# Chunked attention, MoE and routed MoE on one core: ones spread on the chip, `a` loaded once, the first unit's states emitted sooner, and 64 small products of zeros around TensorE's first work

## Chip, cores and metric

One Trainium2 chip, one core. The metric is device time in microseconds (us) of one execution. Each kernel is run several times; the profile is of one more execution of the same program, and its rows are in microseconds from the start of its span.

## What is computed

Three layers follow one another on 4 x 768 = 3072 tokens. The change lies in the start of the first.

```python
def _attn_ref(x, a, B, C):          # batch 4, 8 heads, 768 steps, head_dim 32, d_state 16, chunks of 32
    log_a = np.log(np.clip(a, 1e-06, 1.0))
    for c in range(nc):
        cum = np.cumsum(la, axis=-1)
        M = (C B^T) * exp(cum_i - cum_j) * causal
        y = M @ x + (C @ state) * exp(cum)
        state = exp(sum(la)) * state + sum_j B_j x_j exp(cum_last - cum_j)
def _moe_ref(x, w_gate, w_val, w_out):      # 256 -> 1536 -> 256
    return silu(x @ w_gate) * (x @ w_val) @ w_out
def _moe2_ref(...):                          # 8 experts, 256 -> 1024 -> 256, top 1
    e_idx = np.argmax(x @ w_gate + modality_bias[modality_id], axis=1)
    out[mask] = gate_w[mask, None] * (np.maximum(x[mask] @ w1[e], 0.0) @ w2[e])
```

## The kernel before

The tokens lie in 6 blocks of 512. A block has 4 units of 128 steps (`NU` = 24 units), and a unit holds all 8 heads. The attention of a unit is built from small TensorE products: `scores_mm` (lines 293 and 299) makes the sums for the state and the scores `pc`, `scores_m` (307) masks the scores, `states` (317 to 329) carries the state, `values_mm` (345 and 355) makes `py`, `values_out` (371 to 376) multiplies by the decays `U` and rounds into `xt`, and `values_low` (382) keeps the remainder of that rounding. Weights of the first MLP come as 64-bit numbers in strips of 768 KB (`load_w`, line 393) and are taken apart by `decode`: ScalarE makes `ha` (405) and `wv` (408), VectorE joins them (414, then 418), ScalarE makes the high part `wh` (421), VectorE or GpSimd the low part `wl` (423). The MLP's products (`mlp1_mm`, line 443) can begin when block 0's `xt` and strip 0 are complete.

`first_block` (from line 808) writes out by hand the order in which every engine gets its work, under a manual schedule. It loads, takes the logarithm of `a` (`setup_ln`, 184 and 185), makes the decay weights `W` (`setup_decay`, 189 and 190) and the running sums `er` (`setup_cum`, 196 and 198), weighs unit 0 with `W` (`weigh`, 280) and then goes through the four units of block 0, with four, four and six idle products (`keep_busy`, 207) in between. `cum_split` (225, 228) splits `er`, `setup_ones` (217, 218) copies two matrices of ones out of the constants `c1`, `emit_d` (261, GpSimd) spreads `er` into `du`, `emit_u` (272, 273) multiplies `du` by the ones into `U`, and `cum_ends_d`, `cum_ends` and `cum_store` (233, 240, 245) make the factors `eb` that `states` needs.

Loads are issued from SyncE (SP) in the order of the code; `c1` is issued from ScalarE in two pieces. `at` holds `a` twice side by side, because `setup_cum` wants both copies as its stationary operand. `raw` has three buffers, for the weight strips. PSUM tiles come from pools: tag `a` with 3 buffers (`pc`, `py`), tag `g` with 3 (`pw`, `pe`, `pu`, later the MLP), and two `y` banks, one of which `keep_busy` writes.

Of the kernel before, what the change touches and what calls it, by code (L numbers as in the profile page):

```python
# [9 lines left out]
F32 = mybir.dt.float32  # L10
# [20 lines left out]
NBLK = T // BLK  # L31
# [5 lines left out]
C_S = 0  # L37
C_ME = C_S + 132
C_MU = C_ME + 1
C_R16 = C_MU + 8  # L40
C_R32 = C_R16 + 128
C_MK = C_R32 + 256
C1 = C_MK + 64
C_ID = C1
C_TRI = C_ID + 128
# [9 lines left out]
def _consts():  # L55
    k = np.arange(128)[:, None]
    j = np.arange(128)[None, :]
    c = np.zeros((128, C_END), np.float32)

    same = k // 64 == j // 64  # L60
    m = np.zeros((128, 128), np.float32)
    m[same & (k % 64 < 32) & (k > j)] = 1.0
    m[same & (k % 64 >= 32) & (k <= j)] = -1.0
    c[:, C_S:C_S + 128] = m
    for q, (lo, hi) in enumerate(((32, 96), (96, 128), (0, 32))):
        c[lo:hi, C_S + 128 + q] = -1.0
    r = np.arange(128)
    c[:, C_ME] = (r // 32) % 2
    for q in range(8):
        c[:, C_MU + q] = 4 * (r // 64) + (r // 8) % 4 == q  # L70
    c[:, C_R16:C_R16 + 128] = (r % 8)[:, None] == j // 16
    for g in range(2):
        c[:, C_R32 + 128 * g:C_R32 + 128 * g + 128] = (r % 8)[:, None] == 4 * g + j // 32
    c[:, C_MK:C_MK + 64] = j[:, :64] >= k % 64
    c[:, C_ID:C_ID + 128] = k == j
    c[:, C_TRI:C_TRI + 128] = k < j
    e = np.arange(E)
    c[:, C_IE:C_IE + 8] = 8 - e
    for g, (b0, n) in enumerate(GROUPS):
        c[:, C_EC + 8 * g:C_EC + 8 * g + 8] = E * b0 * BLK + e * (n * BLK)  # L80
    c[:, C_LE:C_LE + 64] = (e[None, :] <= e[:, None]).reshape(1, 64)
    c[:, C_TT:C_TT + 11] = np.arange(11)
    c[:, C_KK:C_KK + 4] = np.arange(4) * BLK
    c[:, C_IO:C_IO + 8] = e
    return c


def _layout(inp):
    o = {}
    at = inp["a"].reshape(NB * NH, NC, 128).reshape(NB, NH, NC, 128).transpose(3, 0, 2, 1)  # L90
    at = at.reshape(128, NBLK, 1, 32)
    o["at"] = np.broadcast_to(at, (128, NBLK, 2, 32)).reshape(128, NBLK, 64)
    xk = inp["x"].reshape(NB, NH, NC, 128, D).transpose(3, 0, 2, 1, 4).reshape(128, NU, DM)
    bk = inp["B"].reshape(NB, NH, NC, 128, N).transpose(3, 0, 2, 1, 4).reshape(128, NU, 128)
    bt = inp["B"].reshape(NB, NH, NC, 128, N).transpose(1, 4, 0, 2, 3).reshape(128, NU, 128)
    o["xbb"] = np.concatenate([xk, bk, bt], axis=2)

    ct = inp["C"].reshape(NB, 2, 4, NC, 2, 64, N).transpose(1, 2, 6, 0, 3, 4, 5).reshape(2, 4, N, NU, 2, 64)
    cd = np.zeros((2, 4, N, NU, 2, 4, 64), np.float32)
    for h in range(4):  # L100
        cd[:, h, :, :, :, h] = ct[:, h]
    o["cbd"] = cd.reshape(128, NU, 512)
    o["cst"] = _consts()

    def bits(w):
        return np.ascontiguousarray(w).view(np.int64)

    wg = bits(inp["moe_w_gate"]).reshape(2, 128, NF, 128).transpose(2, 1, 0, 3)
    wv = bits(inp["moe_w_val"]).reshape(2, 128, NF, 128).transpose(2, 1, 0, 3)
    wo = bits(inp["moe_w_out"]).reshape(NF, 128, DM)  # L110
    o["mw"] = np.concatenate([wg.reshape(NF, 128, 256), wv.reshape(NF, 128, 256), wo], axis=2)
    o["mid"] = np.ascontiguousarray(inp["moe2_modality_id"]).reshape(NU, 128).T
    o["wl"] = inp["moe2_w_gate"].reshape(2, 128, E).transpose(1, 0, 2)
    o["mb"] = np.broadcast_to(inp["moe2_modality_bias"].reshape(1, 2, E), (128, 2, E))
    w1 = inp["moe2_w1"].reshape(E, 2, 128, F2).transpose(0, 2, 1, 3).reshape(E, 128, 2 * F2)
    w2 = inp["moe2_w2"].reshape(E, NF2, 128, DM).transpose(0, 2, 1, 3).reshape(E, 128, NF2 * DM)
    o["ew"] = np.concatenate([w1, w2], axis=2).reshape(E * 128, 4096)
    return {k: np.ascontiguousarray(v) for k, v in o.items()}
# [3 lines left out]
def kernel(  # L122
# [23 lines left out]

    c1 = ap_.tile([128, C1], F32, name="c1")
    c2 = keep.tile([128, C_END - C1], F32, name="c2")
    at = ap_.tile([128, NBLK, 64], F32, name="at")
    W = ap_.tile([128, NBLK, 32], F32, name="W")  # L150
    eb = ap_.tile([128, NU, 4], F32, name="eb")
    er = ap_.tile([128, NBLK // 2, 132], F32, name="er")
# [10 lines left out]
    def load(u):  # L163
        if u >= NU or u in raw:
            return
        r = {}
        xbb = ap_.tile([128, 512], F32, name="xbb", tag="xbb", bufs=4)
        nc.sync.dma_start(out=xbb, in_=I["xbb"][:, u])
        r["x"] = xbb[:, 0:DM].rearrange("k (h d) -> k h d", h=8)
        r["b"] = xbb[:, DM:DM + 128]  # L170
        r["bt"] = xbb[:, DM + 128:]
        r["c"] = ap_.tile([128, 2, 4, 64], F32, name="cbd", tag="cbd", bufs=4)
        nc.sync.dma_start(out=r["c"].rearrange("p r h i -> p (r h i)"), in_=I["cbd"][:, u])
        raw[u] = r

    def setup_loads():
        nc.sync.dma_start(out=at[:, 0:2], in_=I["at"][:, 0:2])
        nc.scalar.dma_start(out=c1[:, 0:C_R16], in_=I["cst"][:, 0:C_R16])
        nc.scalar.preload_act_table_set("natural_log_exp_and_others")
        nc.scalar.dma_start(out=c1[:, C_R16:C1], in_=I["cst"][:, C_R16:C1])  # L180

    def setup_ln(b0, b1):
        a = at[:, b0:b1]
        nc.vector.tensor_scalar(out=a, in0=a, scalar1=1e-6, scalar2=1.0, op0=ALU.max, op1=ALU.min)
        nc.scalar.activation(out=a, in_=a, func=AF.Ln)

    def setup_decay(b0, b1):
        p = ps_g("pw", (128, b1 - b0, 32))
        nc.tensor.matmul(out=p, lhsT=c1[:, C_S:C_S + 128], rhs=at[:, b0:b1, 0:32], start=True, stop=True)
        nc.scalar.activation(out=W[:, b0:b1], in_=p, func=AF.Exp)  # L190

    def setup_cum(b0, n):

        p = ps_g("pe", (128, n, 132))
        for b in range(n):
            nc.tensor.matmul(out=p[:, b], lhsT=at[:, 2 * (b0 + b):2 * (b0 + b) + 2].rearrange("k b c -> k (b c)"),
                             rhs=c1[:, C_S:C_S + 132], start=True, stop=True)
        nc.scalar.activation(out=er[:, b0:b0 + n], in_=p, func=AF.Exp, scale=-1.0)

# [2 lines left out]
    def keep_busy(n):  # L202
# [3 lines left out]
        for _ in range(n):  # L206
            nc.tensor.matmul(out=idle_t[0], lhsT=r32[:, 0],
                             rhs=r32.rearrange("p g j -> p (g j)").unsqueeze(1).to_broadcast([128, 2, 256]),
                             start=True, stop=True)

    def silu_first():

        t = ap_.tile([128, 1], F32, name="sf")
        nc.scalar.activation(out=t, in_=c1[:, C_ME:C_ME + 1], func=AF.Silu)

    def setup_ones():
        nc.vector.tensor_copy(out=r16, in_=c1[:, C_R16:C_R16 + 128])
        nc.vector.tensor_copy(out=r32, in_=c1[:, C_R32:C_R32 + 256].rearrange("p (g j) -> p g j", g=2))

    def cum_split(b0, n):  # L220

# [22 lines left out]
    def cum_store(b0, n, p):  # L244
        nc.vector.tensor_copy(out=eb[:, 8 * b0:8 * b0 + 8 * n], in_=p)

    def cum_pairs(u0, u1):

        nc.vector.tensor_tensor(out=eb[:, u0:u1, 3], in0=eb[:, u0 - 1:u1 - 1, 1], in1=eb[:, u0:u1, 2], op=ALU.mult)
# [25 lines left out]
    def weigh(u, e):  # L275

        r = raw[u]
        b, o = divmod(u, 4)
        r["xw"] = ap_.tile([128, 8, 32], F32, name="xw", tag="xw", bufs=3)
        e.tensor_tensor(out=r["xw"], in0=r["x"], in1=W[:, b, o * 8:o * 8 + 8].unsqueeze(2).to_broadcast([128, 8, 32]),  # L280
                        op=ALU.mult)
# [21 lines left out]
    def scores_m(u):  # L303
        r = raw[u]
        r["m"] = ap_.tile([128, 2, 4, 64], F32, name="mt", tag="mt", bufs=2)
        for g in range(2):
            nc.vector.tensor_tensor(out=r["m"][:, g], in0=r["pc"][g][:, 0:256].rearrange("p (h i) -> p h i", h=4),  # L307
                                    in1=mk.unsqueeze(1).to_broadcast([128, 4, 64]), op=ALU.mult)
# [80 lines left out]
    def load_w(f, e=nc.sync):  # L389
        if f >= NF:  # L390
            return
        wr[f] = keep.tile([128, 768, 2], I32, name="wraw", tag="raw", bufs=3)
        e.dma_start(out=wr[f], in_=I["mw"][f].bitcast(I32).rearrange("p (n t) -> p n t", t=2))
# [415 lines left out]
    def first_block():  # L809
# [1 line left out]
        setup_loads()  # L811
        load(0)
        load(1)
        nc.sync.dma_start(out=at[:, 2:], in_=I["at"][:, 2:])
        load_w(0)
        load(2)
        load(3)
        load_w(1)
        setup_ln(0, 2)
        setup_decay(0, 2)  # L820
        setup_cum(0, 1)
        weigh(0, nc.vector)
        scores_mm(0)
        cum_split(0, 1)
        setup_ones()
        scores_m(0)
        emit_u(0, emit_d(0))
        weigh(1, nc.gpsimd)
        cum_store(0, 1, cum_ends(0, 1, cum_ends_d(0, 1)))
        states(0)  # L830
        cum_pairs(1, 8)
        setup_ln(2, NBLK)
        decode(0, 0)
# [303 lines left out]
```

## Time and profile before

| what | us |
|---|---|
| three timed runs | 534.32, 530.82, 531.13 |
| their median | 531.13 |
| the profiled execution's own time | 530.68 |
| its span | 528.9 |
| TensorE (PE) busy in it | 504.5 (95%) |
| VectorE (DVE) busy | 290.0 (55%) |
| ScalarE (ACT) busy | 219.6 (42%) |
| GpSimd (POOL) busy | 106.6 (20%) |

The span is what the profiler saw of the engines; the 1.8 us around it belong to the execution but to no row. In rows, PE is a product, PEld its weight load, SPq the issue of a DMA by SyncE. A row of the timeline begins with its start and its length; in brackets at its end stands how long the engine had been idle before it, and what ended that. "issue" means that the engine waited for nothing that the profile shows.

### The profile page before, as it was taken

What the parts mean: (1) busy time and instruction counts of PE and PEld (TensorE: products, weight loads), DVE (VectorE), ACT (ScalarE), POOL (GpSimd) and SP (SyncE); (2) the same over time, 40 slices, a digit from 0 to 9 for tenths busy, and PEclk for the clock granted to TensorE, in tenths of its full rate; (3) what the DMA queues carried; (4) which work ended last, traced back from release to release, by engine and by line L of the source; (5) the groups of instructions that cost most, each with busy time, mean ns of one, the idle gap of its engine ahead of it and who ended that gap; (6) DMA issues with size and microseconds to landing.
All of it is one profiled execution on the core that took longest, in us unless ns stands there. A gap on an engine that the chain in (4) does not pass through costs nothing.

```text
span 528.9 us, 11246 instructions
## 1 busy us (share of the span) xinstructions
PE 504.5 (95%) x4580; PEld 416.9 (79%) x4580; DVE 290.0 (55%) x631; ACT 219.6 (42%) x403; POOL 106.6 (20%) x127
## 2 busy tenths in 40 slices
PE   5889999999999999999999999999999999999990
PEld 3577787788778778888788778888899989999880
DVE  4898776944554544445444554455466564646320
ACT  3785575533333324233333232434454353534220
POOL 3200000221220130005000124211047426240220
PEclk9999999999999999999999999999999999999996
DMA  8954422021231312012100104234197544531100
GB/s 314 313 196 149 160 68 86 29 52 41 82 30 33 103 13 66 5 43 80 21 2 2 43 1 157 85 121 41 41 104 181 157 130 136 154 103 42 40 22 22
DMA packets 20838, 45.84 MB, mean 87 GB/s; under 512 B 4656, under 2 KB 8496, under 8 KB 20784
## 3 DMA queue, kind: packets, MB, share of 16 engines
q1 hardware_dynamic: 17424, 38.39, 26.1%
q0 software_dynamic: 3072, 6.41, 3.8%
q8 instruction: 37, 0.61, 0.6%
q10 hardware_dynamic: 288, 0.30, 0.2%
q14 instruction: 17, 0.14, 0.1%
HBM read 38.59 MB, written 6.50 MB: 85 GB/s over the span
## 4 chain that ended last, share of the span: by engine, by line
PE 78%; issue 9%; DVE 5%; ACT 3%; POOL 2%; DMA 1%; SPq 0%; POOLq 0%; DVEq 0%
PE py L471 19%; PE pg L443 18%; PE pv L443 18%; PE ph L760 8%; PE po L781 8%; PE pt L555 2%; PE pc L299 2%; POOL out L795 1%; PE py L355 1%; PE py L345 1%; DMA cbd<-in_cbd 1%; PE px L749 1%; PE pc L293 1%; DVE mt L307 1%; DVE wv L414 1%
## 5 line engine op out<-in xcount | busy, mean ns | idle before, releaser
L443 PE MATMUL pg<-xt,wh 128*128 128x512 f32 x288 | 93.1, 404 | 1.0 <-ACT xt L376 0.9
L443 PE MATMUL pv<-xt,wh 128*128 128x512 f32 x288 | 90.3, 395 | 0.0
L451 DVE TENSOR_TENSOR h<-h,pv 128x512 f32<-128x512 f32 x72 | 49.3, 685 | 65.7 <-PE pv L443 56.8
L458 DVE TENSOR_TENSOR hl<-h,hh 128x512 fp32r<-128x512 f32 x72 | 50.4, 700 | 61.7 <-ACT hh L457 61.5
L760 PE MATMUL ph<-xt,hl 128*128 128x512 f32 x288 | 72.7, 394 | 0.0
L781 PE MATMUL po<-hl,hh 128*128 128x256 f32 x384 | 70.2, 283 | 0.0
L443 PEld LDWEIGHTS pv<-xt,wh 128*128 128x128 f32 x288 | 54.2, 188 | 12.8
L781 PEld LDWEIGHTS po<-hl,hh 128*128 128x128 f32 x384 | 60.3, 188 | 2.1
L443 PEld LDWEIGHTS pg<-xt,wh 128*128 128x128 f32 x288 | 52.2, 189 | 12.2 <-ACT xt L376 1.3
L457 ACT CAST hh<-h 128x512 fp32r<-128x512 f32 x72 | 44.6, 620 | 40.4 <-DVE h L451 40.4
L616 POOL DMA_INDIRECT slots<-ids,si x24 | 25.9, 1081 | 168.4 <-DVE si L608 163.6
L450 ACT ACTIVATE h<-pg 128x512 f32<-128x512 f32 x72 | 42.7, 593 | 41.0 <-PE pg L443 41.0
L760 PEld LDWEIGHTS ph<-xt,hl 128*128 128x128 f32 x288 | 51.7, 188 | 9.2
L471 PE MATMUL py<-hh,wh 128*128 128x512 f32 x144 | 58.6, 407 | 0.0
L443 PE MATMUL pg<-xt,wl 128*128 128x512 f32 x144 | 57.0, 396 | 0.3 <-DVE wl L423 0.3
L471 PE MATMUL py<-hl,wh 128*128 128x512 f32 x144 | 56.9, 395 | 0.0
L471 PE MATMUL py<-hh,wl 128*128 128x512 f32 x144 | 56.8, 395 | 0.0
L443 PE MATMUL pv<-xt,wl 128*128 128x512 f32 x144 | 56.8, 394 | 0.0
L781 PE MATMUL po<-hl,hl 128*128 128x256 f32 x192 | 53.9, 281 | 0.2 <-DVE hl L769 0.2
L769 DVE SCALAR_TENSOR_TENSOR hl<-ph,hh 128x512 fp32r<-128x512 f32 x48 | 33.0, 688 | 32.9 <-ACT hh L768 32.8
L768 ACT ACTIVATE hh<-ph 128x512 fp32r<-128x512 f32 x48 | 28.8, 600 | 42.9 <-PE ph L760 27.6
L781 PEld LDWEIGHTS po<-hl,hl 128*128 128x128 f32 x192 | 36.1, 188 | 0.4 <-DVE hl L769 0.4
(140 smaller groups left out, 670.8 us busy)
## 6 DMA issues: line engine op xcount, KB each, us to landing
eraw<-in_ew SPq DMA_DIRECT2D x24, 512.0 KB, 3.8
wraw<-in_mw SPq DMA_DIRECT2D x12, 768.0 KB, 4.5
xbb<-in_xbb SPq DMA_DIRECT2D x24, 256.0 KB, 4.6
cbd<-in_cbd SPq DMA_DIRECT2D x24, 256.0 KB, 4.5
yd<-yr SPq DMA_DIRECT2D x6, 528.0 KB, 3.3
slots<-ids,si POOLq DMA_INDIRECT x24, 9.0
xg<-yd,idx POOLq DMA_INDIRECT x24, 3.8
out<-ob,idx POOLq DMA_INDIRECT x24, 2.5
```

Of the source, the lines that this page charges most:

```text
L299: nc.tensor.matmul(out=r["pc"][g][32 * q:32 * q + 32, 0:256], lhsT=r["bt"][k, 32 * q:32 * q + 32], rhs=r["c"][k, q // 2].rearrange("p h i ...
L443: nc.tensor.matmul(out=t, lhsT=w[:, f, o:o + 128], rhs=xt[:, xp, k, cs], start=n == 0, stop=n == 5)
L450: nc.scalar.activation(out=h, in_=p[0], func=AF.Silu)
L451: nc.vector.tensor_tensor(out=h, in0=h, in1=p[1], op=ALU.mult)
L457: nc.scalar.copy(out=hh, in_=h)
L458: e.tensor_tensor(out=hl, in0=h, in1=hh.bitcast(F32), op=ALU.subtract)
L471: nc.tensor.matmul(out=yb[b][d][:, c:c + m], lhsT=w[:, f, o:o + 128], rhs=h, start=first and n == 0, stop=last and n == 2, skip_group_chec ...
L616: i = nc.gpsimd.indirect_dma_start(out=slots[0:E * upto], out_offset=bass.IndirectOffsetOnAxis(ap=si[:, s:s + 1], axis=0), in_=ids[g][:, o ...
L760: nc.tensor.matmul(out=p, lhsT=self.hl[:, w, o:o + 128], rhs=self.xt[:, xp, k], start=n == 0, stop=n == 5)
L768: nc.scalar.activation(out=hh, in_=p, func=AF.Relu)
L769: nc.vector.scalar_tensor_tensor(out=hl, in0=p, scalar=0.0, in1=hh.bitcast(F32), op0=ALU.max, op1=ALU.subtract)
L781: nc.tensor.matmul(out=self.po[s // 2][:, s % 2], lhsT=h[:, q], rhs=self.hl[:, w, o:o + DM], start=f == 0 and n == 0 and s % 2 == 0, stop= ...
```

## The change

Constants: the two matrices of ones (128 and 256 columns) are no longer loaded; `c1` holds 8 columns in their place, which `setup_ones` spreads by broadcast. With that `c1` is 213 columns, not 589, and one DMA. `a` is loaded once into `at0` (half the bytes), and the clipping step writes it twice into `at`. `load(2)` is issued ahead of `load_w(0)`. `cum_ends_d` and `cum_ends` stand ahead of `scores_m(0)`, unit 1 is weighed by GpSimd ahead of `emit_d(0)`, and `emit_u(0)` stands behind `states(0)`. A new function issues bfloat16 products of zeros, 64 columns wide with 32 stationary columns: 50 ahead of the first work of TensorE, 14 between `setup_cum` and `scores_mm(0)`.

```diff
-C_R16 = C_MU + 8
-C_R32 = C_R16 + 128
-C_MK = C_R32 + 256
+C_P8 = C_MU + 8
+C_MK = C_P8 + 8
...
-    at = at.reshape(128, NBLK, 1, 32)
-    o["at"] = np.broadcast_to(at, (128, NBLK, 2, 32)).reshape(128, NBLK, 64)
+    o["at"] = at.reshape(128, NBLK, 32)
...
     def setup_loads():
-        nc.sync.dma_start(out=at[:, 0:2], in_=I["at"][:, 0:2])
-        nc.scalar.dma_start(out=c1[:, 0:C_R16], in_=I["cst"][:, 0:C_R16])
+        nc.sync.dma_start(out=at0[:, 0:2], in_=I["at"][:, 0:2])
+        nc.scalar.dma_start(out=c1, in_=I["cst"][:, 0:C1])
         nc.scalar.preload_act_table_set("natural_log_exp_and_others")
-        nc.scalar.dma_start(out=c1[:, C_R16:C1], in_=I["cst"][:, C_R16:C1])
...
-        nc.vector.tensor_scalar(out=a, in0=a, scalar1=1e-6, scalar2=1.0, op0=ALU.max, op1=ALU.min)
+        nc.vector.tensor_scalar(out=a, in0=at0[:, b0:b1].unsqueeze(2).to_broadcast([128, b1 - b0, 2, 32]),
+                                scalar1=1e-6, scalar2=1.0, op0=ALU.max, op1=ALU.min)
...
+    def warm_up(n):
+
+        if not warm_t:
+            warm_t.append(ap_.tile([128, 64], BF16, name="zb"))
+            nc.vector.memset(warm_t[0], 0.0)
+            idle_t.append(ps.tile([128, 2, 256], F32, tag="y0", bufs=1, name="pi"))
+        for _ in range(n):
+            nc.tensor.matmul(out=idle_t[0][0:32, 0, 0:64], lhsT=warm_t[0][:, 0:32], rhs=warm_t[0],
+                             start=True, stop=True)
...
     def setup_ones():
-        nc.vector.tensor_copy(out=r16, in_=c1[:, C_R16:C_R16 + 128])
-        nc.vector.tensor_copy(out=r32, in_=c1[:, C_R32:C_R32 + 256].rearrange("p (g j) -> p g j", g=2))
+        p8 = c1[:, C_P8:C_P8 + 8].unsqueeze(2)
+        nc.vector.tensor_copy(out=r16.rearrange("p (h n) -> p h n", h=8), in_=p8.to_broadcast([128, 8, 16]))
+        nc.vector.tensor_copy(out=r32.rearrange("p g (h i) -> p (g h) i", h=4), in_=p8.to_broadcast([128, 8, 32]))
...
         load(0)
         load(1)
-        nc.sync.dma_start(out=at[:, 2:], in_=I["at"][:, 2:])
+        nc.sync.dma_start(out=at0[:, 2:], in_=I["at"][:, 2:])
+        load(2)
         load_w(0)
-        load(2)
         load(3)
         load_w(1)
+        warm_up(50)
         setup_ln(0, 2)
         setup_decay(0, 2)
         setup_cum(0, 1)
+        warm_up(14)
         weigh(0, nc.vector)
         scores_mm(0)
         cum_split(0, 1)
         setup_ones()
+        weigh(1, nc.gpsimd)
+        d = emit_d(0)
+        p = cum_ends(0, 1, cum_ends_d(0, 1))
         scores_m(0)
-        emit_u(0, emit_d(0))
-        weigh(1, nc.gpsimd)
-        cum_store(0, 1, cum_ends(0, 1, cum_ends_d(0, 1)))
+        cum_store(0, 1, p)
         states(0)
+        emit_u(0, d)
```

SyncE's queue at the start of the program, before (the first DMA is `a` of block 0 and 1; `wraw` is strip 0):

```order
L177 DMA at_71<-in_at 128x128
L168 DMA xbb_95<-in_xbb 128x512
L173 DMA cbd_97<-in_cbd 128x512
L168 DMA xbb_99<-in_xbb 128x512
L173 DMA cbd_101<-in_cbd 128x512
L814 DMA at_71<-in_at 128x256
L393 DMA wraw_104<-in_mw 128x1536
L168 DMA xbb_106<-in_xbb 128x512
L173 DMA cbd_108<-in_cbd 128x512
```

The same queue now:

```order
L174 DMA at0_71<-in_at 128x64
L165 DMA xbb_95<-in_xbb 128x512
L170 DMA cbd_97<-in_cbd 128x512
L165 DMA xbb_99<-in_xbb 128x512
L170 DMA cbd_101<-in_cbd 128x512
L824 DMA at0_71<-in_at 128x128
L165 DMA xbb_104<-in_xbb 128x512
L170 DMA cbd_106<-in_cbd 128x512
L403 DMA wraw_108<-in_mw 128x1536
```

Strip 0 has moved behind the two loads of unit 2, and the two loads of `a` are half as wide.

TensorE's first rows before, up to the decays of unit 0 (`pe_165` is the product of `cum_ends`, `pu` that of `emit_u`):

```order
L189 MATMUL pw<-at,c_69 128x64
L196 MATMUL pe<-c_69,at 128x132
L293 MATMUL pc<-xw,xbb 32x64 x8
L299 MATMUL pc<-cbd,xbb 32x256 x8
L272 MATMUL pu<-du,r_76 128x512 x2
L240 MATMUL pe_165<-d_163,r_75 128x32
```

The same place now, from the last of the 14 products of zeros on:

```order
L217 LDWEIGHTS zb
L217 MATMUL pi<-zb 32x64
L303 MATMUL pc<-xw,xbb 32x64 x8
L309 MATMUL pc<-cbd,xbb 32x256 x8
L250 MATMUL pe_222<-d_220,r_76 128x32
L282 MATMUL pu<-du,r_77 128x512 x2
```

The product of `cum_ends` has passed the two of `emit_u`, and with the 64 pairs of a weight load and a product 128 instructions stand ahead of everything that follows.

## Rows read from the trace of the kernel before

**Rows 1.** Windows: stretch, length, busy us (instructions) of PE, PEld, DVE, ACT, POOL; PEclk, DMA share, GB/s
```profile
0.00:25.00 25.00, 16.80 (x429) 11.41 (x429) 15.89 (x49) 14.44 (x30) 7.24 (x12) 1.00 0.90 318
25.00:50.00 25.00, 23.51 (x342) 18.29 (x343) 22.80 (x52) 15.68 (x29) 0.00 (x0) 1.00 0.57 196
50.00:100.00 50.00, 49.65 (x393) 39.57 (x392) 38.44 (x69) 32.17 (x57) 3.53 (x10) 1.00 0.26 90
```
**Rows 2.** Timeline of DVE, 8 to 26 us: start, length, operation [idle before, what ended it]
```profile
8.27 0.91 DVE L233 TENSOR_TENSOR d<-er,c 128x32 fp32r<-128x32 f32 x1
...
14.03 0.96 DVE L414 SCALAR_TENSOR_TENSOR wv<-ha,wv 128x768 int32<-128x768 int32 x1 [0.27 <-ACT wv L408]
...
18.50 0.42 DVE L382 TENSOR_TENSOR xt<-y,xt 128x256 fp32r<-128x256 f32 x1 [0.35 <-ACT xt L376]
...
21.35 1.21 DVE L414 SCALAR_TENSOR_TENSOR wv<-ha,wv 128x768 int32<-128x768 int32 x1
...
25.03 0.42 DVE L382 TENSOR_TENSOR xt<-y,xt 128x256 fp32r<-128x256 f32 x1 [0.47 <-ACT xt L376]
```
**Rows 3.** Timeline of ACT, 8 to 26 us
```profile
10.81 0.42 ACT L185 ACTIVATE at<-at 128x256 f32<-128x256 f32 x1 [1.29 <-DVE at L184]
11.14 0.91 ACT L405 ACTIVATE ha<-wraw 128x768 f32<-128x768 f32 x1
...
12.81 0.35 ACT L329 ACTIVATE st<-sv,eb 128x64 f32<-128x64 f32 x1 [0.53 <-DVE sv L323]
13.07 0.93 ACT L408 ACTIVATE wv<-wraw 128x768 int32<-128x768 uint32 x1
...
16.86 0.28 ACT L190 ACTIVATE W<-pw 128x128 f32<-128x128 f32 x1 [1.61 <-PE pw L189]
```
**Rows 4.** DMA issues of 0 to 30 us: out<-in, queue, count, KB each, us to landing
```profile
c<-in_cst ACTq DMA_DIRECT2D x1, 224.0 KB, 4.5
...
at<-in_at SPq DMA_DIRECT2D x1, 128.0 KB, 5.0
c<-in_cst ACTq DMA_DIRECT2D x1, 70.5 KB, 2.4
at<-in_at SPq DMA_DIRECT2D x1, 64.0 KB, 2.2
```
**Rows 5.** DMA issues of 3.5 to 5.4 us: strip 0 and the second load of unit 2
```profile
wraw<-in_mw SPq DMA_DIRECT2D x1, 768.0 KB, 6.4
...
cbd<-in_cbd SPq DMA_DIRECT2D x1, 256.0 KB, 6.0
```
**Rows 6.** Timeline of SP: when strip 0 and the second load of unit 2 were issued
```profile
3.53 0.70 SPq L393 DMA_DIRECT2D wraw<-in_mw  x1
...
5.28 0.33 SPq L173 DMA_DIRECT2D cbd<-in_cbd  x1
```
**Rows 7.** Windows: 3 to 12 us, columns as in the first group
```profile
3.00:12.00 9.00, 6.37 (x113) 3.91 (x118) 4.15 (x15) 3.07 (x8) 3.34 (x4) 1.00 1.01 379
```
**Rows 8.** Timeline of all engines, TensorE's rows: first work, scores of unit 0, second logarithm block
```profile
3.56 0.69 PE L189 MATMUL pw<-at,c 128*128 128x64 f32 x2 [3.56 <-ACT at L185]
...
6.40 1.11 PE L299 MATMUL pc<-cbd,xbb 64*32 64x256 f32 x16
...
16.44 0.38 PE L189 MATMUL pw<-at,c 128*128 128x128 f32 x2 [1.51 <-issue]
...
17.02 1.18 PE L207 MATMUL pi<-r 128*128 128x512 f32 x4
```
**Rows 9.** Windows: between two waits of TensorE for "issue", columns as in the first group
```profile
16.43:21.23 4.80, 4.56 (x125) 3.30 (x125) 4.34 (x15) 4.20 (x10) 1.95 (x2) 1.00 0.97 334
```
**Rows 10.** Line 299 in 0 to 13 us, then in 13 to 24 us: ns min/median/max
```profile
L299 PE MATMUL pc<-cbd,xbb x32: 627/631/632, 6.4 to 11.1; 64*32 64x256 f32 x32
...
L299 PE MATMUL pc<-cbd,xbb x48: 376/376/400, 13.6 to 21.5; 64*32 64x256 f32 x48
```
**Rows 11.** Timeline of PE, 140.6 to 140.8 us: narrow bfloat16 products of the router
```profile
140.68 0.24 PE L598 MATMUL pr<-oh,oneb 128*128 128x32 bf16 x4
```

More of the change, by code (lines that the diff above doesn't have):

```diff
@@ L70, in _consts @@
         c[:, C_MU + q] = 4 * (r // 64) + (r // 8) % 4 == q
-    c[:, C_R16:C_R16 + 128] = (r % 8)[:, None] == j // 16
-    for g in range(2):
-        c[:, C_R32 + 128 * g:C_R32 + 128 * g + 128] = (r % 8)[:, None] == 4 * g + j // 32
+    c[:, C_P8:C_P8 + 8] = (r % 8)[:, None] == np.arange(8)[None, :]
     c[:, C_MK:C_MK + 64] = j[:, :64] >= k % 64
@@ L148 @@
     c2 = keep.tile([128, C_END - C1], F32, name="c2")
-    at = ap_.tile([128, NBLK, 64], F32, name="at")
+    at0 = ap_.tile([128, NBLK, 32], F32, name="at0")
+    at = ap_.tile([128, NBLK, 2, 32], F32, name="at")
     W = ap_.tile([128, NBLK, 32], F32, name="W")
@@ L188, in setup_decay @@
         p = ps_g("pw", (128, b1 - b0, 32))
-        nc.tensor.matmul(out=p, lhsT=c1[:, C_S:C_S + 128], rhs=at[:, b0:b1, 0:32], start=True, stop=True)
+        nc.tensor.matmul(out=p, lhsT=c1[:, C_S:C_S + 128], rhs=at[:, b0:b1, 0], start=True, stop=True)
         nc.scalar.activation(out=W[:, b0:b1], in_=p, func=AF.Exp)
@@ L195, in setup_cum @@
         for b in range(n):
-            nc.tensor.matmul(out=p[:, b], lhsT=at[:, 2 * (b0 + b):2 * (b0 + b) + 2].rearrange("k b c -> k (b c)"),
+            nc.tensor.matmul(out=p[:, b], lhsT=at[:, 2 * (b0 + b):2 * (b0 + b) + 2].rearrange("k b t c -> k (b t c)"),
                              rhs=c1[:, C_S:C_S + 132], start=True, stop=True)
@@ L209, in keep_busy @@
                              start=True, stop=True)
+    warm_t = []
+    def warm_up(n):
[6 more added lines that the diff above has]
+                             start=True, stop=True)
     def silu_first():
```

## Prediction

> **What bounds the kernel now.** I read the windows first. In [rows 1] TensorE is busy 16.80 of the first 25 us, 23.51 of the next 25 and 49.65 of the 50 after that; the page has it at 95% of the span. So from about 50 us on nothing but TensorE counts, and nothing in the change touches that part. What can be won lies before the first product of the MLP, which starts when unit 3's remainder is rounded, at 25.03 [rows 2]. Between 25 and 50 us VectorE is busy 22.80 of 25 us: it works off the decode of the strips while TensorE waits a little for it. A prologue that ends a microsecond sooner therefore moves VectorE's and TensorE's work alike, and I count each microsecond before 25 us as one of the total.
>
> The timelines of VectorE and ScalarE come next, because they are dense from 14 us on. VectorE starts on strip 0 at 14.03 and had waited 0.27 us for ScalarE's `wv`; it waits again 0.35 us at 18.50 and 0.47 at 25.03 [rows 2]. So the time of `wv` sets the start of this dense stretch, and the first unit's own work on VectorE was done at 13.76. ScalarE comes to `wv` at 13.07 by `ha` at 11.14; between them it waits 0.53 us for unit 1's state [rows 3]. Before `ha` it had waited for the second logarithm (10.81, idle 1.29), which VectorE clips only after unit 0's states. Strip 0 itself had landed at 3.53 + 6.4 = 9.93 [rows 5, 6], 1.2 us before it was used.
>
> Last the DMA. From 3 to 12 us its engines are busy all the time (share 1.01) and move 379 GB/s [rows 7]. In this stretch an order of loads is an order of landings.
>
> **Bytes and the order of loads.** `a` goes from 64.0 + 128.0 KB to half, 96 KB less; the constants from 70.5 + 224.0 KB to 213/589 of it, 106.5, so 188 KB less [rows 4]. Together 284 KB or 291,000 bytes, at 379 GB/s 0.77 us for everything that lands behind them. Strip 0 now comes after both loads of unit 2. The set of loads up to there is the same as before, and its last one landed at 5.28 + 6.0 = 11.28 [rows 5, 6]. So strip 0 lands at 11.28 - 0.77 = 10.5, later than the old 9.93 by 0.6 us, but before `ha` began (11.14).
>
> **The first unit's chain.** Unit 0's scores start at 6.40 and take 1.11 us, to 7.51 [rows 8]. The small product behind `eb` could not start before 9.18, because VectorE reached its operand only at 8.27, behind the masking, and the instruction took 0.91 us [rows 2]. Now it stands ahead of the masking, and the product stands right behind the scores, at 7.5: up to 1.7 us sooner for `eb`, the states, the second logarithm and unit 1's scores, which wait for a PSUM buffer that the states free. Moving unit 1's weighing ahead of `du` on GpSimd and `emit_u` behind the states delays `U`; behind `U` wait the second logarithm and `ha` on ScalarE, and I count on both being clear of it when strip 0 lands at 10.5. The two casts that spread the ones keep their shapes on the output side; I cost them at nothing, since VectorE waits for unit 0's scores right behind them.
>
> **Start of the dense stretch.** With the state ready, `ha` to `wv` takes 13.07 - 11.14 - 0.53 = 1.40 us. So `wv` starts at 10.5 + 1.4 = 11.9, and VectorE on strip 0 at 11.9 + (14.03 - 13.07) = 12.86, against 14.03: 1.17 us won. The condition is that the first unit is off VectorE by then; it was done at 13.76, so it must win 0.9 of its 1.7 us, and 0.8 are to spare. Bounds: if the smaller loads save no time, strip 0 lands at 11.28 and 0.4 us is left; if strip 0 never binds, the whole 1.7 us. I take 1.17, the strip's own arithmetic.
>
> **TensorE's wait for "issue".** Before its second logarithm block TensorE waited 1.51 us although nothing in the trace held it [rows 8], and for that ScalarE stood idle 1.61 us at 16.86 [rows 3]; VectorE's 0.35 us at 18.50 is what came of it. TensorE waits for "issue" again at 21.23, and between the two it ran 125 products and 125 loads in 4.80 us [rows 9]. I read this as code that arrives in blocks, of which the next was late. The 64 added pairs are 128 instructions, about half such a block, so these waits move: the one before the logarithm falls away, and others come half a block earlier and later. Off the 0.35 I count 0.2 (ScalarE's own chain to the next `wv` takes the rest), with 0 and 0.82 as bounds (both VectorE waits gone). For a late block in unit 3, ahead of the six idle products, I add 0.2, with 0 and 1.5 as bounds (the whole old wait on the path).
>
> The Trainium skill, "Runtime: NRT & Kernel Launch", section "Instruction fetch mechanics", says that code is fetched in blocks of 256 instructions and that crossing a block is mostly hidden. The trace agrees on the size and not on the hiding here. By that page a fetch costs nothing, both 0.2 fall away, and the sum stays; the rival of a late block below would have no chance.
>
> **The 64 products of zeros.** The trace has no such row. Four narrow bfloat16 products of the router take 0.24 us together, 0.06 each [rows 11]; idle products of 512 columns step at 1.18/4 = 0.295 us, which for 64 columns is 0.037 [rows 8]. The granted clock stands at 1.00 (the 2.4 GHz level) in every stretch of [rows 1], yet line 299 takes 631 ns up to 11.1 us and 376 ns from 13.6 us on [rows 10]: I take it that TensorE worked as at the 1.2 GHz level up to 11.1 us and at 2.4 GHz from 13.6 us. At the lower level the two prices are 1.68 times as much, 0.062 and 0.10. Fully in series a pair could cost 0.24 x 1.68 = 0.40. I take 0.07, near the idle products, since 50 in a row hide their own fill: 4.5 us. There is room for them: TensorE has no work until 3.56 and starts the scores at 6.40; from about 1.0 us (an estimate, VectorE has to clear the tile first) and without some 1.1 us for the first two groups of products (an estimate from the 0.69 us of the first), that is 4.3 us. The 0.2 over comes out of the 0.8 to spare, so the products cost nothing. What they give, a higher clock before 13 us, shortens legs that strip 0 hides.
>
> **Sum.** 530.68 - 1.17 - 0.2 + 0.2 = 529.5 us. The profiled execution lies 0.45 under the median of the runs shown (531.13) and 0.14 under the fastest (530.82), so on the scale of the median it would be 529.9. I give 529.5; the likeliest case by itself spans 528.8 to 530.2.
>
> **Rivals.**
> A late block or late strip eats it. The strip lands at 11.28, or the half-block shift puts the whole 1.5 us where unit 3 or the MLP waits: 529.5 + 0.8 to 529.5 + 1.3, so 530.3 to 530.8. For it speak the wait of 1.51 us that is there today [rows 8] and a DMA that has no slack; against it that unit 3's work ends in six idle products which hold nothing.
>
> More is won. Strip 0 does not bind, the chain gives its 1.7, VectorE's two waits go (0.82), 2.5 us: 528.2, and 527.7 if some of TensorE's 1.5 idle us between 25 and 50 [rows 1] shrink too. Against it: strip 0 comes 0.6 us later by its new place in the queue, in a stretch where the queue is full. The page "TensorE: Matmul & The Clock Gate" of the Trainium skill, Part 1, says that the low clock is the default and activity lifts it; the lengths of line 299 agree [rows 10], and whether products of zeros count as such shows no run here.
>
> Slower: the products of zeros run over. Everything of block 0 stands behind them on TensorE, the first decay weights too. They are free up to 4.3 + 0.8 = 5.1 us, 0.08 us a pair; from 5.1 + 1.2 = 6.3 us, 0.098 a pair, the gain is gone. At 0.15 a pair, 9.6 us, the kernel is 3.3 us slower: 534.0. For it speaks the price of the router's products at the lower level, 0.10, and that all 64 write one place in PSUM; against it that the idle products write one place too and step without a gap [rows 8].
>
> **Chances.** Forecast 0.60, eaten 0.18, more won 0.13, slower than before 0.09. The range from 527.9 to 531.7 leaves out the overrun and the best of the larger gain, and takes in that runs of one kernel scatter by a few tenths. A measurement of this kernel can tell a change of about 1%, 5.3 us. A larger gain than that has no row (0.02); a larger loss needs 0.18 us a pair (0.03); within 1% is 0.95.
>
> **What would show it.** Right: `ha` starts when strip 0 lands, near 10.5; VectorE's line of the first join starts near 12.9 and the MLP's first product near 23.9; TensorE's wait ahead of the second logarithm is gone. Wrong: the products of zeros end later than 6.6 us; strip 0 lands after 11.2; a wait for "issue" of over 1 us stands between unit 2's values and the MLP; or the MLP starts 1.2 us sooner and the total does not follow, which would say that the stretch from 25 to 50 us gives it back.

## The result and the profile after

The changed kernel takes 539.33 us (median of 4 runs, 536.94 to 541.4); the kernel before, on the same chip, 530.98 (4 runs). The ratio is 1.0147, 95% interval 1.0108 to 1.0185: slower, by 8.4 us. Forecast were 529.5 us, within 527.9 to 531.7. The profiled execution of after is the slowest of its four, 541.4 us with a span of 539.5, so the rows below add up to 10.6 us rather than 8.4.

TensorE's list of waits (line, what ended them, us in total, times, longest) shows where to look first:

```profile
PE py L365 <- issue: 4.7, 1, 4.7
PE py L355 <- DVE sv L333: 2.6, 1, 2.6
PE py L481 <- DVE yT L553: 2.0, 1, 2.0
PE pu L282 <- POOL du L271: 1.8, 1, 1.8
PE pi L217 <- DVE zb L214: 0.9, 1, 0.9
PE pu L282 <- DVE sv L333: 0.9, 1, 0.9
```

Before, the one large wait for "issue" was 1.51 us [rows 8]. Now there is one of 4.7 us. The second line is of the same kind: the list blames VectorE's `sv`, but on the row below the weight loads of those products ended their wait on "issue". TensorE's timeline of after (start, length, operation, idle before):

```profile
0.95 2.85 PE L217 MATMUL pi<-zb 128*32 128x64 bf16 x50 [0.95 <-DVE zb L214]
3.72 0.69 PE L186 MATMUL pw<-at,c 128*128 128x64 f32 x2
...
4.89 0.85 PE L217 MATMUL pi<-zb 128*32 128x64 bf16 x14
5.67 0.34 PE L303 MATMUL pc<-xw,xbb 64*32 64x64 f32 x16
5.81 0.64 PE L309 MATMUL pc<-cbd,xbb 64*32 64x256 f32 x16
...
15.88 0.35 PEld L355 LDWEIGHTS py<-mt,xw 64*32 64x32 f32 x23 [2.75 <-issue]
15.91 0.57 PE L355 MATMUL py<-mt,xw 64*32 64x64 f32 x23 [2.62 <-DVE sv L333]
...
28.30 0.47 PE L365 MATMUL py<-cbd,st 64*32 64x64 f32 x16 [4.66 <-issue]
28.70 0.80 PE L204 MATMUL pi<-r 128*128 128x512 f32 x1
...
161.80 0.50 PE L481 MATMUL py<-hh,wh 128*128 128x512 f32 x1 [1.99 <-DVE yT L553]
```

The products of zeros are a little cheaper than forecast and are over as the scores begin. They also do what was left open about them: the scores' second group takes 0.64 us, where it took 1.11 [rows 8]. The loss comes later. Both long waits stand inside a group of products of one unit: 23 of L355 behind the first, the last 16 of L365 behind the second. Nothing in the data separates those from the products ahead of them.

VectorE and ScalarE of after, the rows that answer to [rows 2, 3]:

```profile
11.45 0.91 ACT L415 ACTIVATE ha<-wraw 128x768 f32<-128x768 f32 x1 [1.00 <-DMA wraw<-in_mw]
...
13.67 0.96 DVE L424 SCALAR_TENSOR_TENSOR wv<-ha,wv 128x768 int32<-128x768 int32 x1 [0.76 <-ACT wv L418]
...
28.85 0.36 DVE L381 TENSOR_TENSOR y<-py,U 128x192 f32<-128x192 f32 x1 [3.62 <-PE py L365]
...
30.20 0.42 DVE L392 TENSOR_TENSOR xt<-y,xt 128x256 fp32r<-128x256 f32 x1 [0.47 <-ACT xt L386]
```

The first join starts at 13.67 instead of 14.03 (12.86 was forecast), and the rounding of unit 3's remainder, which the MLP waits for, at 30.20 instead of 25.03 [rows 2]. The MLP's first product follows at 31.43, against 25.05 before: 6.4 us late. The windows of after, columns as in [rows 1], say the same for the engines:

```profile
0.00:25.00 25.00, 18.26 (x471) 13.71 (x472) 14.67 (x46) 13.15 (x27) 7.28 (x12) 0.86 0.78 266
25.00:50.00 25.00, 21.26 (x340) 16.43 (x339) 19.37 (x44) 14.94 (x25) 0.00 (x0) 0.86 0.55 186
50.00:100.00 50.00, 49.65 (x403) 39.49 (x392) 37.92 (x72) 30.08 (x55) 0.00 (x0) 1.00 0.34 116
...
10.00:12.00 2.00, 2.00 (x66) 1.46 (x50) 1.13 (x4) 1.00 (x3) 0.17 (x1) 0.50 1.06 424
...
16.00:18.00 2.00, 2.00 (x66) 1.83 (x67) 1.04 (x6) 0.17 (x1) 0.61 (x1) 0.50 0.09 29
...
26.00:32.00 6.00, 3.69 (x24) 2.85 (x24) 2.64 (x10) 1.23 (x5) 0.00 (x0) 0.50 0.48 147
```

Between 25 and 50 us TensorE is busy 21.26 us where it was 23.51, VectorE 19.37 where it was 22.80 [rows 1]: the dense stretch has a hole. The granted clock is 0.50 (the 1.2 GHz level) from 16 to 18 us and from 26 to 32, each time after TensorE had stood still, so that the first products of the MLP take longer as well (the third 0.63 us, against 0.39 before). The rest of the loss is far from the change: 2.0 us at 161.80, slower products behind it (0.63 us instead of 0.39 for three of L481) and 0.9 us near 270. 6.4 + 2.0 + 0.9 = 9.3 of 10.6; I did not itemize the remainder, to which the slower products behind 161.80 belong.

**When the code arrives.** The queue that carries TensorE's instructions (`q8`) moves 16 KB at a time: 38 packets in the whole execution, for 9,288 products and loads, 244 each. I read a packet as a block of code, and take it that the packet for the next block is asked for about one block, some 250 instructions, ahead of the place where TensorE would stop without it; for the two long waits these places are at 5.8 and 20.6 us. The DMA view of after (queue, packets, MB, share), first 20.6 to 25.7 us and then 25.7 to 26.8:

```profile
q1 hardware_dynamic: 487, 1.68, 95.3%
...
q1 hardware_dynamic: 222, 0.40, 95.6%
q8 instruction: 1, 0.02, 5.6%
```

For five microseconds the load queue holds its engines 95% busy and no code comes; the packet follows at 25.76, with the queue still as busy, and TensorE goes on at 28.30, 1.5 us after that stretch. The other wait reads alike: no packet from 5.8 to 13.2 us, one between 13.2 and 14.4, and TensorE goes on at 15.88. Where the queue is nearly empty (share 6.6% from 15.5 to 16.9 us) a packet comes between 16.9 and 18.1 and nothing waits for it. Between the ends of the two waits lie 252 products and 253 loads, two blocks of some 250:

```profile
15.87:28.29 12.42, 7.73 (x252) 6.18 (x253) 6.83 (x18) 7.06 (x14) 3.15 (x3) 0.77 0.70 231
```

Theory A: the 128 added instructions moved the ends of the blocks by half a block, to places where TensorE runs through a block in some 3 us (20.6 to 23.6, ahead of the second wait) while the packet for the next waits behind loads. Theory B: the products of zeros cost by themselves, by their work or by the clock that follows them.

### The profile page after: what moved, and what is told of

The parts are those of the page before. It is cut to its first block, busy times and chain, and to the rows that moved or that the text cites. A ratio compares the mean times of both kernels' runs of the same rounds, so it can differ in the third digit from the quotient of the medians.

```text
span 539.5 us, 11372 instructions
## 1 busy us (share of the span) xinstructions
PE 511.5 (95%) x4644; PEld 423.1 (78%) x4644; DVE 290.2 (54%) x632; ACT 219.1 (41%) x403; POOL 105.4 (20%) x127
## 3 DMA queue, kind: packets, MB, share of 16 engines
q1 hardware_dynamic: 17424, 38.29, 25.7%
## 4 chain that ended last, share of the span: by engine, by line
PE 75%; issue 11%; DVE 5%; POOL 2%; DMA 2%; ACT 2%; SPq 1%; POOLq 0%; DVEq 0%; ACTq 0%
PE py L481 18%; PE pg L453 18%; PE pv L453 17%; PE ph L770 6%; PE po L791 6%; PE pt L565 2%; POOL out L805 2%; PE pc L309 1%; PE py L365 1%; PE py L355 1%; DMA wraw<-in_mw 1%; PE pi L204 1%; PE pc L303 1%; DVE wv L424 1%; DVE hl L468 1%
## 5 line engine op out<-in xcount | busy, mean ns | idle before, releaser
L481 PE MATMUL py<-hh,wh 128*128 128x512 f32 x144 | 58.9, 409 | 2.0 <-DVE yT L553 2.0
L481 PE MATMUL py<-hl,wh 128*128 128x512 f32 x144 | 57.2, 397 | 0.0
L481 PE MATMUL py<-hh,wl 128*128 128x512 f32 x144 | 57.0, 396 | 0.0
```

What stands on the lines that cost most here:

```text
L481: nc.tensor.matmul(out=yb[b][d][:, c:c + m], lhsT=w[:, f, o:o + 128], rhs=h, start=first and n == 0, stop=last and n == 2, skip_group_chec ...
```

## The experiments

All ratios are to the kernel before, run on the same chip (530.4 to 530.8 us).

**Without the products of zeros.**

```
-        warm_up(50)
...
-        warm_up(14)
```

> The changed kernel without the 64 products of zeros; all else stays. Theory A (code: the 128 added instructions move the ends of TensorE's blocks of code to places where the next block is late, 2.6 us near 15.9 us and 4.7 us near 28.3 us): 529 to 531 us, one wait for issue of about 1.5 us back ahead of the second logarithm, none over 1 us after it. Theory B (clock: the products of zeros bring TensorE into a swing between both levels): also near 530 us, but then it is the clock rows that change. Theory C (strip 0 comes too late in its new place in the queue): still 536 us or more, with ha waiting for its landing at 11.4 us.

Measured 530.25 us, ratio 0.9996 (0.9982 to 1.001). All of the loss is gone with the 64 products, and of the forecast gain nothing is left in the medians. The wait ahead of the second logarithm is back with 0.7 us (about 1.5 was expected). Its waits and three rows of its timelines:

```profile
PE pw L186 <- ACT at L182: 3.5, 1, 3.5
PE pc L303 <- DVE mt L317: 1.5, 1, 1.5
PE pu L282 <- POOL du L271: 1.0, 1, 1.0
PE pc L309 <- issue: 0.9, 1, 0.9
PE pw L186 <- issue: 0.7, 1, 0.7
```

```profile
11.36 0.91 ACT L415 ACTIVATE ha<-wraw 128x768 f32<-128x768 f32 x1 [0.64 <-DMA wraw<-in_mw]
...
13.57 0.96 DVE L424 SCALAR_TENSOR_TENSOR wv<-ha,wv 128x768 int32<-128x768 int32 x1 [0.53 <-ACT wv L418]
...
24.42 0.96 PE L453 MATMUL pg<-xt,wh 128*128 128x512 f32 x2 [0.31 <-ACT xt L386]
```

Strip 0 lands at 11.36 and not at 10.5; `ha` waits for it 0.64 us. The MLP starts 0.63 us sooner than before, and this one execution is 0.64 us shorter (530.04 against 530.68), no more than executions of one kernel differ among themselves.

**The products of zeros alone, in the kernel before.** Its edit is the function `warm_up` and its two calls.

> The kernel before with the 64 products of zeros and nothing else of the change. Theory A: 535 to 540 us, with waits for issue of TensorE of several us before the MLP begins. Theory B: slow too, by the low clock in the rows. Theory C: 531 us, as before.

Measured 538.09, ratio 1.015 (1.0133 to 1.0166): with the run above, the two parts add up, and the loss is that of the products. The waits are the changed kernel's in other sizes, 2.8 us at L367 and 2.2 at L357 for "issue", 2.3 at L483 near 159 us.

**The same columns in few instructions.** 6 and 2 products of 512 columns, 4,096 columns as before, in 16 instructions instead of 128.

```
-        for _ in range(n):
-            nc.tensor.matmul(out=idle_t[0][0:32, 0, 0:64], lhsT=warm_t[0][:, 0:32], rhs=warm_t[0],
+        for _ in range(n):
+            nc.tensor.matmul(out=idle_t[0][0:32], lhsT=warm_t[0][:, 0, 0:32], rhs=warm_t[0],
...
-        warm_up(50)
+        warm_up(6)
...
-        warm_up(14)
+        warm_up(2)
```

> The changed kernel with 8 products of zeros of 512 columns (6 and 2) in place of 64 of 64 columns: the same columns in all, 16 instructions in place of 128. Theory A: 529 to 531 us, the waits for issue as in the kernel without zeros. Theory B: 536 to 541 us, the same swing of the clock, since TensorE does the same columns in the same stretch. Theory C: 536 us or more.

Measured 530.9, ratio 1.0008 (0.9997 to 1.002). The work of the zeros costs nothing that can be measured: the 8 products take 3.78 us together, the 64 took 3.70. The granted clock falls here as well, to 0.64 from 10 to 12 us and 0.51 from 12 to 14, and that does not show in the total either, which speaks against the clock half of theory B. Not all is alike, though: L309 of the first unit takes 1.09 us here, not 0.64.

**The same instructions with hardly any work.** 64 products of 2 columns.

```
-            nc.tensor.matmul(out=idle_t[0][0:32, 0, 0:64], lhsT=warm_t[0][:, 0:32], rhs=warm_t[0],
+            nc.tensor.matmul(out=idle_t[0][0:32, 0, 0:2], lhsT=warm_t[0][:, 0:32], rhs=warm_t[0][:, 0:2],
```

> The changed kernel with 64 products of zeros 2 columns wide: all 128 instructions, a thirtieth of the columns. Theory A: 535 to 541 us with the long waits for issue near 16 and 28 us. Theory B: about 530 us, since TensorE does hardly any work ahead of its first. Theory C: 536 us or more.

Measured 534.94, ratio 1.0107 (1.0069 to 1.0144). TensorE's waits and the end of the long one:

```profile
PE py L365 <- issue: 3.0, 1, 3.0
PE pu L282 <- POOL du L271: 1.7, 1, 1.7
PE py L481 <- DVE yT L553: 1.6, 1, 1.6
```

```profile
24.25 0.45 PE L365 MATMUL py<-cbd,st 64*32 64x64 f32 x16 [3.03 <-issue]
24.63 2.93 PE L204 MATMUL pi<-r 128*128 128x512 f32 x6
27.35 0.82 PE L453 MATMUL pg<-xt,wh 128*128 128x512 f32 x2
```

The wait ends on the same product, the first of the last 16 of L365, as in the changed kernel. With the run before this one it decides for theory A: columns without instructions cost nothing, instructions without columns cost 4.5 us. It is not all of the loss: thin products lose 4.5 us, those of 64 columns 7.7 to 8.4. Of the 2.6 us wait at L355 only 0.2 is left here: TensorE ran the last two products ahead of that place at 13.93 and not at 13.02, and the packet came at 12.1 and not at 13.3. Why the packet came sooner is not shown.

**Loads out of the way of the code.** The changed kernel whole, with strip 3 and the second half of the constants asked for after unit 3's work.

```
-                load_w(3)
-                nc.sync.dma_start(out=c2, in_=I["cst"][:, C1:C_END])
...
         decode(2, 0, "t")
+        load_w(3)
+        nc.sync.dma_start(out=c2, in_=I["cst"][:, C1:C_END])
         load_w(4)
```

> The changed kernel with its 64 products of zeros kept, but strip 3 and the second half of the constants asked for later (951.5 KB out of the queue between 17.5 and 22 us). Theory A (the late code blocks wait behind the loads that are in the queue when they are asked for): the code packet that came at 25.76 us comes near 22.5 to 23.5, TensorE's wait for issue of 4.7 us at L365 shrinks to 1 to 2.5 us, the MLP starts before 29.5 instead of 31.43, and the total is 535.5 to 537.5. Theory B (the length of the wait is TensorE's own, whatever is loaded): the wait stays 4 to 5 us and the total 538.5 to 540.

Measured 535.25, ratio 1.0078 (1.0054 to 1.0101): about 3.6 of the 8.4 us are gone. The DMA view from 18 to 22 us and from 22 to 23.1, and TensorE's timeline:

```profile
q1 hardware_dynamic: 382, 1.22, 89.0%
...
q1 hardware_dynamic: 164, 0.29, 71.5%
q8 instruction: 1, 0.02, 5.2%
```

```profile
24.54 0.38 PE L365 MATMUL py<-cbd,st 64*32 64x64 f32 x16 [2.92 <-issue]
27.58 0.89 PE L453 MATMUL pg<-xt,wh 128*128 128x512 f32 x2
```

With 951.5 KB less in the queue the packet comes 3.7 us sooner and the wait is 2.9 us instead of 4.7 (1 to 2.5 was expected). That does not show that the loads set its length. The MLP starts 3.85 us sooner than in the changed kernel, but 1.85 of that lies in the wait at L355, which ended before the deferred loads would have been asked for (0.77 us here, 2.62 there); TensorE is thus 2.2 us sooner at the place where the next block is asked for (18.4 against 20.6). And the thin kernel, which has all of those loads in the queue, waits 3.03 us at the same product, no longer than here: either way other loads kept the queue some 90% busy. The run without zeros and with the same loads later, below, is the cleaner test.

**Strip 0 first in line, without the zeros.**

```
-        load(2)
         load_w(0)
+        load(2)
```

> The change without the 64 products, and strip 0 asked for ahead of unit 2 again, as in the kernel before. Theory A (only the strip's place in the queue kept the gain of the prologue away): the strip lands by 10.6, ha starts by 10.9 and not at 11.36, VectorE's first join at or before 13.1 and not at 13.57, the MLP at 24.0 or sooner, and the total is 529.0 to 529.9. Rival: the states, the logarithm or the codes bind behind it anyway, VectorE's join stays within 0.2 us of 13.57 and the total at 530.1 to 530.6.

Measured 530.71, ratio 1.0007 (0.9994 to 1.0021). `ha` starts at 10.66 and no longer waits for the strip, yet VectorE's join starts at 13.34, 0.23 us sooner than without the edit: ScalarE has `U` at 9.25 and the second logarithm at 10.21, and `wv` begins at 12.29 behind the states. The strip was 0.6 us too late, but behind it stood a chain that ends only 0.23 us sooner. The rival holds; the edit brought besides 2.0 us of "issue" at L309 and the MLP at 26.47, of which the median shows nothing (the profiled execution took 531.52 us).

**Half as many, and twice as many.** One call ahead of TensorE's first work, products of 2 columns, in two kernels.

```
-        warm_up(50)
+        warm_up(32)
...
-        warm_up(14)
```

> 32 products of zeros of 2 columns, all ahead of TensorE's first work (64 instructions). Theory A (what counts is where the ends of code blocks fall and how long the packets for them are under way): the ends move half as far as with 64 products, to places where the packet is nearly there, so the waits for issue stay under 1 us each, and the total is 530 to 531.5. Rival (a product of zeros has its price, 4.5 us by 64 in the run of thin products): 532.5.

> 128 products of zeros of 2 columns ahead of TensorE's first work (256 instructions). Theory A: a whole block is added, so the ends fall on the same products as without zeros, but the first packet is asked for at about 4 us, with the queue full, and comes near 12; waits of 2 to 3 us in unit 1's values near 11 to 14 us and 0 to 3 us in unit 3, none at 154 us; total 532 to 535.5. Rival (a product of zeros has its price): 530.25 + 2 x 4.5 = 539.3.

Measured 530.7 (1.0011, 1.0 to 1.0022) with 32 and 531.21 (1.0016, 1.0005 to 1.0027) with 128, against 534.94 with 64. The cost does not grow with the number; it depends on where the block ends fall, as theory A has it, and a whole block of 256 instructions puts them back: with 128 products TensorE's two waits for "issue" end on L186 of the second logarithm and on L309 of unit 3, the same products as without zeros. The sizes of the waits were missed in both. With 32 there were two waits for "issue" at L365, 2.8 us in all, and the total did not feel them. With 128 the wait near 11 to 14 us did not come, since the first packet was there between 6.6 and 7.8 us and not at 12; of the two only the one at L309 is over 1 us (2.1), and the total came out below the range.

**Loads later, without the zeros.** The two edits above, products out and strip 3 later, together.

> The change without the 64 products and with strip 3 and the second half of the constants asked for later. If what is left of TensorE's waits for issue (0.7 and 0.9 us without the products) also comes from packets behind loads, and the prologue passes it on: packets near 23 us, waits under 0.3 us each, the MLP at 23.5 to 24.1 instead of 24.42 and a total of 529.2 to 529.9. Rival: VectorE's dense stretch sets the start of the MLP whatever TensorE waits for: the MLP within 0.2 us of 24.42, the total 530.0 to 530.6.

Measured 531.34, ratio 1.0017 (1.0007 to 1.0027): neither expectation; of the first only the packet came true (22.5 us, near 23 was expected). The waits for "issue" stay at 1.0 and 0.7 us, and the MLP starts at 24.68. Where the block ends lie well, there is nothing to win this way.

But beside the run without zeros this one shows what the loads do to a packet. In both TensorE goes on at the same product, the first of L309 in unit 3, at 21.18 us there and at 21.12 here. The next packet, which neither had to wait for, came 2.6 us after that with the loads in the queue and 1.4 us after it without them. The DMA views without zeros from 21.2 to 23.7 us and from 23.7 to 24.8:

```profile
q1 hardware_dynamic: 535, 0.96, 103.7%
...
q1 hardware_dynamic: 148, 0.29, 105.0%
q8 instruction: 1, 0.02, 5.6%
```

With the loads later, from 21.1 to 22.5 us and from 22.5 to 23.6:

```profile
q1 hardware_dynamic: 157, 0.28, 55.9%
...
q1 hardware_dynamic: 23, 0.04, 20.7%
q8 instruction: 1, 0.02, 5.3%
```

**The loss at 160 us.** It is in every kernel with 128 added instructions and in none with 0, 16, 64 or 256. But those kernels also come to that place late. Two kernels put 64 thin products into the MLP instead, with nothing in the prologue:

```
+            if i == 2:
+                thin_late(64)
             p = mlp1_mm(b, 0, BLK, f)
```

> The change without its products of zeros, but with 64 thin products (2 columns) ahead of the products of pass 2 of the MLP, near 36 us: the prologue keeps its block ends, all ends behind it shift by 128 instructions. Theory A (a block end inside the unit near 149 us of the kernel before holds TensorE's signals there, and is a loss apart from those of the prologue): MLP starts at 24.4 as without the products; some 1 us for the products themselves; VectorE's line 381 near 150 us waits 3 us or more and TensorE loses 1.5 to 2.5 us behind it; total 532.5 to 534. Rival (the loss at 154 us is an echo of the late prologue): no such wait, total 530.7 to 531.7.

> The same 64 thin products ahead of pass 23, behind the unit in question, so that the block ends up to there stay where they are. Theory A: no wait of 3 us at line 381 near 150 us; only the products themselves, total 530.7 to 531.7, that is 1.5 to 2.5 us under the kernel with the products at pass 2. Rival: both the same within 0.5 us.

Measured 537.52 (1.0138, 1.0114 to 1.0161) and 535.7 (1.0095, 1.008 to 1.011). Both say little: TensorE waited 5.5 and 3.8 us for VectorE to clear the products' tile, and pass 23 begins at 138 us, ahead of the unit in question, so that the second was no control. Both show the loss (2.1 and 2.0 us at L489). The repair clears the tile in the first microsecond and separates shift from lateness:

```
+    zl = keep.tile([128, 128], BF16, name="zl")
...
+        nc.vector.memset(zl, 0.0)
         setup_loads()
...
+            if i == 2:
+                thin_late(64)
```

> No products of zeros in the prologue; 64 thin ones (2 columns, 128 instructions) ahead of pass 2 of the MLP, their tile cleared in the first microsecond, so that nothing waits for it. Theory A (half a block of shift puts a block end into the unit at 154 us, and TensorE's signals there come late): TensorE loses 1 to 2 us near 36 us and 1.5 to 2.5 us more at 154 us, with VectorE's wait of 3 us or more at the join of that unit; total 533 to 534.5. Theory C (the loss at 154 us follows whenever TensorE comes several us late to that unit, through the route's scatters on GpSimd): with so little lateness no loss there, total 531 to 532.

> 128 products of zeros of 128 columns ahead of pass 2 (256 instructions, a whole block): TensorE comes 6 to 8 us later to everything behind, but the block ends fall where they fell. Theory A: no loss at 154 us, VectorE waits under 1 us at the join of that unit; total 536 to 538.5, all of it from 36 us. Theory C: the loss of 1.5 to 2.5 us at 154 us comes as well, total 538 to 541.

Measured 534.23 (1.0076, 1.0056 to 1.0096) and 536.83 (1.0118, 1.0101 to 1.0135). The join of the unit on VectorE and the next wait of TensorE, with 64 thin products:

```profile
152.95 0.36 DVE L389 TENSOR_TENSOR y<-py,U 128x192 f32<-128x192 f32 x1 [3.42 <-PE pg L461]
...
156.04 0.50 PE L489 MATMUL py<-hh,wh 128*128 128x512 f32 x1 [1.70 <-DVE yT L561]
```

With 128 products of 128 columns, which come later to the unit but leave the block ends where they were:

```profile
155.26 0.34 PE L373 MATMUL py<-cbd,st 64*32 64x64 f32 x12
...
155.65 0.36 DVE L389 TENSOR_TENSOR y<-py,U 128x192 f32<-128x192 f32 x1 [0.47 <-PE py L373]
```

Late without a shift: no loss. A shift almost without lateness (the unit's values end 0.9 us later than in the run without zeros): 1.7 us. So it is the place of the block end in that unit that costs there, and not an echo of the prologue. In each of the seven kernels with 128 added instructions VectorE's join begins 2.9 to 4.1 us after the last product that it needs, and 0.5 to 1.5 us after the start of one code packet; in the others it begins 0.05 us after that product. What holds the signals is not shown. In the changed kernel the products' rows run on at their pace from 155 to 158 us, VectorE's L381 starts only at 158.71, and that queue's one code packet between 150 and 159.4 us comes after 158, though the load queue moves nothing from 154.7 to 158.

None of the versions beats the kernel before by more than can be measured.

## Why the prediction was wrong

**The late block: the step that failed.** "For a late block in unit 3, ahead of the six idle products, I add 0.2, with 0 and 1.5 as bounds (the whole old wait on the path)." The place was right, the mechanism too: the block end came into unit 3's last products and ahead of the idle ones. The size was not: 4.66 us there, on the path in full, so that the MLP came 6.4 us late together with the wait in unit 1. The bound took the length of the wait from the one row at hand, 1.51 us, as if it belonged to the block. It differs with what the load queue holds when the code is asked for: after TensorE had gone on, a packet came in 1.1 us with that queue at 6.6%, in 1.4 at 56% and in 2.6 at 104%, and 5.1 us passed at 95%. What makes the difference between the last two is not shown. The rows for a wider bound were there: the DMA share of 0.97 in the stretch between the two waits [rows 9]. By an estimate from those rows one strip of 768 KB alone takes 2.4 us at 334 GB/s, so a bound of several microseconds was called for. Two of the prediction's own signs of being wrong came: strip 0 after 11.2, and a wait for "issue" of over 1 us ahead of the MLP.

**"the one before the logarithm falls away, and others come half a block earlier and later".** That was right as far as the place goes: L186 follows at 17.00 with nothing in the list of waits. But the one that came half a block earlier, 2.62 us in unit 1, has no term in the sum, which counts the old wait as 0.2 us won. The Trainium skill, "Runtime: NRT & Kernel Launch", section "Instruction fetch mechanics", has crossing a block mostly hidden. For the MLP the runs agree: from 50 to 100 us TensorE runs 403 products and 392 loads in 50 us, about 16 a microsecond, and waits for no code. In the units it is not so: 125 products and 125 loads in 4.80 us [rows 9] are 52 a microsecond, and in such stretches TensorE waited up to 4.7 us.

**"nothing in the change touches that part".** This too failed, for the time from 50 us on: the 128 instructions moved a block end into the unit near 155 us, and TensorE lost 2.0 us at 161.80 and ran slower products behind it. The sum has no term for it.

**The products of zeros.** Right on their price: 50 in 2.85 us, 0.057 each, against the 0.07 taken. The rival of the overrun, the only one that I had for "slower", failed on its mechanism: it looked at the time that the products take, and that time is free, as the wide ones show (3.78 us). What cost was their count of instructions, by where it put the block ends: 128 thin ones cost less than 64.

**What they give.** "What they give, a higher clock before 13 us, shortens legs that strip 0 hides" holds: L309 takes 0.64 us for the first unit, and `ha` then waits 1.00 us for strip 0. By the Trainium skill, "TensorE: Matmul & The Clock Gate", Part 1, activity lifts the clock. The trace agrees, and products of zeros do count here, though the first unit's L309 took 1.09 us behind the 8 wide ones and 1.11 behind the thin ones. The gain does not last: in 10 to 12 us the granted clock of after is 0.50, and it falls again after each of the long waits.

**Strip 0.** "0.77 us for everything that lands behind them" failed. 284 KB less were in the queue, and the strip landed at 11.36 in the kernel without zeros, not at 10.5; the prediction's own bound for loads that save no time was 11.28. The DMA moved 351 GB/s from 3 to 12 us where it had moved 379 [rows 7]; why is not shown. Nor would an earlier strip have given the rest: with the strip first in line the join still began at 13.34, held by ScalarE's own chain.

**"I count each microsecond before 25 us as one of the total".** For small shifts this is not settled. Against the profiled execution of before, the MLP starts 0.63 us sooner without the zeros and that execution is 0.64 us shorter; with the strip first it starts 1.4 us later and the execution is 0.8 us longer; with the loads later it starts 0.4 us sooner and the execution is 0.5 us longer. Large delays did come through: 6.4 us of the changed kernel's loss.

## What to carry to other kernels

Count instructions, not only time: products put into a gap for nothing still push the ends of code blocks, and a block end that falls into a dense run of small instructions while the load queue is full cost several microseconds here. Before adding some, look where TensorE waits for "issue", how fast it uses its code there, and how much is in the load queue; here a few wide products, or a whole block of 256 instructions, filled the gap without the loss. And bound a stall by what it waits for, not by the one stall of its kind in the profile.

## What the runs showed of the hardware

- A code packet of 16 KB waits with the loads: none came for 7.4 us (5.8 to 13.2) and for 5.1 us (20.6 to 25.7) with the load queue at 95% and more; with that queue at 6.6% one came 1.1 us after TensorE had gone on. Between two kernels that go on at the same product at the same time, the packet came in 2.6 us with the queue at 104% and in 1.4 us at 56%.
- TensorE went on 1.6 us after the packets of both long waits had passed, not at once.
- Fewer bytes did not land sooner: the loads up to strip 0 and unit 2 were in at 11.28 us before and at 11.36 in the kernel without zeros, with 284 KB less and 351 instead of 379 GB/s in the same 9 us.
- In each of the seven kernels with 128 added instructions, VectorE's join in one unit in the middle of the MLP began 2.9 to 4.1 us after the products that it needs, with an idle load queue and a code packet that started 0.5 to 1.5 us ahead of it. The cause is open.
- The granted clock stood at the 1.2 GHz level behind both long waits of the changed kernel, so that a wait was paid for a second time in slower products.
